# Placing v by small transfers and repeating e on TensorE, in a fused attention and soft-MoE kernel

## The chip, the cores and the metric

The kernel runs on one core of a Trainium2 chip. The time is the device time of one launch in microseconds (us). A core has five engines that run side by side and meet at semaphores: PE (TensorE, matrix products; its weight loads are listed as PEld), DVE (VectorE), ACT (ScalarE), POOL (GpSimd) and SP (SyncE, which here only issues transfers). Transfers run on 16 DMA engines. A transfer that casts its data is issued by POOL and shows up as queue q0 in the profile; transfers issued by SP are queue q1.

## The reference

```python
def _attn_ref(q, k, v, cap):              # q, k, v: (8, 12, 448, 64) float32
    scores = (1 / sqrt(64)) * q @ k^T
    scores = cap * tanh(scores / cap)     # cap = 30
    attn = softmax(scores)
    return attn @ v

def _moe_ref(x, phi, w1, w2):             # x: (3584, 768), phi: (768, 32)
    logits = x @ phi                      # w1: (8, 768, 1024), w2: (8, 1024, 768)
    d = softmax(logits over tokens)       # per slot
    slot_input = (d.T @ x).reshape(8, 4, 768)
    for e in range(8):
        slot_out[e] = relu(slot_input[e] @ w1[e]) @ w2[e]
    c = softmax(logits over slots)        # per token
    return c @ slot_out
```

The attention output, with its heads side by side, is the `x` of the mixture. All inputs and the output are float32; the kernel computes in bf16 with sums in float32.

## The kernel before

The 96 heads are taken in 24 groups of four, called quads (`Q`). A quad holds two head pairs (`pr = 2 Q + h`), and the two heads of a pair lie on the two halves of the 128 partitions. A pair's 448 keys are cut into 7 pieces of 64, so that one tile of scores has 64 keys of each of two heads on its partitions and 448 queries along the row. Six such tiles make a chunk `j`; there are 56 chunks.

A loop over the chunks is the spine of the kernel. In chunk `j`, ACT takes tanh of two halves of scores (L324) and exp of the chunk before (L328); PE computes the scores of the next chunk (`qk_chunk`, L315) and, for a pair whose exponentials are complete, the product with v (`pv_first`, `pv_tail`, `pv_rest`, L586); DVE normalises it into `xq` (L596) and computes part of the exponentials as polynomials (L560 to L568). The order on each engine is written out by hand: `at(j, slot, f, ...)` hangs further work into a slot of a chunk ("0", "m", "e", "a", "b", "r", "c", "d"), `run(j, slot)` issues it, and a table `WHEN` gives slots for the transposes of k and q (L275), the transposes of x, the logits, the exponentials e of the logits, and their sums. PE also gets matmuls whose result nobody reads (L616, L829, L832).

v enters the product through two block-diagonal tiles, `vbds[0]` and `vbds[1]`, taken in turn by the quads. A row has 2 x 7 pieces of `VW = 130` values: 64 values of v of the first head and a one, then 64 of the second head and a one. On partitions 0 to 63 only the first half of a piece is filled, on 64 to 127 only the second; zeros and ones are written once (`init_vbd`). v is loaded as float32 into one staging tile, `vraw`, in two transfers of 64 partitions (`load_v`, issued by SP, L195), and `vcast` (L285) copies it on POOL into `vbds[Q % 2]`, cast to bf16, one half of the partitions at a time. `vcast_after(pr)`, behind the product of each pair, issues these casts; ahead of one of them POOL writes a zero into one column (L293).

POOL issues all transfers that cast: k and q of later quads (`load`, L185, two tiles of each) and 64 pieces of the weights (`wjobs`): 32 of `w1` and 11 of `w2` into on-chip tiles and 21 of `w2` into a copy in DRAM (`w2d`), which SP reads back behind the attention (`w2t`, L1015). The pieces are spread over the chunks.

Per batch of 12 heads (three quads) there are logits for 32 slots (`phib`, loaded once in 128-byte pieces), and their exponentials `es[b]`, 128 tokens by 4 groups by 32 slots. `e_rep` (L679) copies `es[b]` on POOL four times side by side into `e4s[b]`. `e_norm` (L687) multiplies `e4s` with a column of ones to add up e over the tokens, and `e_transp` (L698) transposes it: in both the four copies land on four blocks of 32 partitions. Behind the attention come the two expert layers (L1036, L1069) and the combination (L1107, L1158), whose results SP stores.

Of the kernel before, what the change touches and what calls it, by code (L numbers as in the profile page):

```python
# [9 lines left out]
F32 = mybir.dt.float32  # L10
BF16 = mybir.dt.bfloat16
# [7 lines left out]
P = 128  # L19
HP = 64  # L20
NT = 7
DH = 64
S = 448
CH = 6
CS = 3
NG = 4
NF = 3
NEX = 5
TAIL = NF * P
W = DH + 1  # L30
# [7 lines left out]
def kernel(  # L38
# [12 lines left out]
    B, H, _, _ = q.shape  # L51
    D = H * DH
    E = moe_w1.shape[0]
    F = moe_w1.shape[2]
    NS = moe_phi.shape[1]
# [7 lines left out]
    NQ = B * NQB  # L63
# [6 lines left out]
    pe, dve, act, pool, sp = nc.tensor, nc.vector, nc.scalar, nc.gpsimd, nc.sync  # L70

    consts = ctx.enter_context(tc.tile_pool(name="consts", bufs=1))
    wts = ctx.enter_context(tc.tile_pool(name="wts", bufs=1))
# [4 lines left out]
    ones = wide[:, 0:P]  # L78
    dve.memset(ones, 1.0)
    ident = consts.tile([P, P], BF16, name="ident")  # L80
# [5 lines left out]
    half1 = consts.tile([P, 1], BF16, name="half1")  # L86
# [55 lines left out]
    ldv, wk = homes["ldv"], homes["wk"]  # L142
# [21 lines left out]
    raws, casts, qkT = {}, {}, {}  # L164
# [3 lines left out]
    def quad_ap(nm, Q, h=None):  # L168
        b, hq = divmod(Q, NQB)
        off = (b * H + 4 * hq) * S * DH  # L170
        if h is not None:
            return bass.AP(tensor=srcs[nm].tensor, offset=off + 2 * h * S * DH,
                           ap=[[NT * DH, P], [1, NT * DH]])
        return bass.AP(tensor=srcs[nm].tensor, offset=off,
                       ap=[[NT * DH, P], [2 * S * DH, 2], [1, NT * DH]])
# [9 lines left out]
            pool.dma_start(out=t, in_=quad_ap(nm, Q))  # L185
            raws[nm, Q] = t

    vraw = ldv.tile([P, 2, S], F32, name="vraw")

    def load_v(Q, n):  # L190

        if Q < NQ:
            r = slice(n * HP, n * HP + HP)
            src = quad_ap("v", Q)
            sp.dma_start(out=vraw[r],  # L195
                         in_=bass.AP(tensor=src.tensor, offset=src.offset + n * S * DH,
                                     ap=[[NT * DH, HP]] + list(src.ap[1:])))
            raws["v", Q] = vraw

    def load_first():  # L200

        for nm in "qk":
            raws[nm, 0] = [ld.tile([P, S], F32, name=f"{nm}raw{h}", tag=nm + "raw", bufs=2)
                           for h in range(2)]
        raws["v", 0] = vraw
        kc = raws["k", 0][0].rearrange("p (c d) -> p c d", d=DH)
        kin = quad_ap("k", 0, 0).rearrange("p (c d) -> p c d", d=DH)
        sp.dma_start(out=raws["q", 0][0], in_=quad_ap("q", 0, 0))
        for c0, c1 in ((0, CS), (CS, NT)):
            act.dma_start(out=kc[:, c0:c1, :], in_=kin[:, c0:c1, :])  # L210
        for nm in "kq":
            sp.dma_start(out=raws[nm, 0][1], in_=quad_ap(nm, 0, 1))
        t = wts.tile([P, 3, 2, S], F32, name="raw1", tag="w1", bufs=E)
        t01 = wts.tile([P, 2, 2, NT, P], BF16, name="casts", tag="w1", bufs=E)
        for n, nm in enumerate("kqv"):
            raws[nm, 1] = t[:, n, :, :]
            if nm != "v":
                for Q in range(2):
                    casts[nm, Q] = t01[:, n, Q, :, :]
            if nm == "v":  # L220
                sp.dma_start(out=raws["v", 0], in_=quad_ap("v", 0))
            sp.dma_start(out=raws[nm, 1], in_=quad_ap(nm, 1))
# [59 lines left out]
    def vcast(Q, n):  # L282
        raw = raws["v", Q].rearrange("p h (c d) -> p h c d", d=DH)
        r, c0 = slice(n * HP, n * HP + HP), n * W
        pool.tensor_copy(vbds[Q % 2][r, :, :, c0:c0 + DH], raw[r])  # L285
        if Q != 1:
            load_v(max(Q + 1, 2), n)

    def vcast_after(pr):

        Q, h = divmod(pr, 2)
        if h == 0 and 1 < Q + 1 < NQ:
            pool.memset(vbds[Q % 2][HP:P, h, NT - 1, 0:1], 0.0)  # L293
            vcast(Q + 1, 1)
        elif h == 1 and Q + 2 < NQ:
            vcast(Q + 2, 0)

    def init_vbd(n):
        t = vbds[n]
# [366 lines left out]
        for hq in range(NQB):  # L666
            xTs.pop(b * NQB + hq)

    es, e4s = {}, {}

    def e_exp(b):
        es[b] = consts.tile([P, NG, NS], BF16, name="E", tag="E", bufs=2)
        act.activation(es[b], lps.pop(b), ACT.Exp)
        e_rep(b)

    def e_rep(b):

        e4s[b] = consts.tile([P, NG, 4 * NS], BF16, name="e4", tag="e4", bufs=1)
        pool.tensor_copy(e4s[b].rearrange("p g (a s) -> p g a s", a=4),  # L679
                         es[b].unsqueeze(2).to_broadcast([P, NG, 4, NS]))  # L680

    def e_norm(b):

        ps = psT.tile([P, 1], F32, name="zps", tag="T")
        for g in range(NG):
            r = slice(0, P if g < NF else HP)
            pe.matmul(ps, e4s[b][r, g, :], ones[r, 0:1], start=(g == 0), stop=(g == NG - 1))  # L687
        if b == 0:
            dve.tensor_copy(zacc, ps)
        else:  # L690
            dve.tensor_tensor(zacc, ps, zacc, op=ALU.add)

    def e_transp(b):

        ps = psT.tile([P, 512], BF16, name="eps", tag="T")
        for g in range(NG):
            n = P if g < NF else HP
            pe.transpose(ps[:, g * P:g * P + n], e4s[b][0:n, g, :], ident[0:n, 0:n])  # L698
        dve.tensor_copy((ETl if b >= B - 2 else ET4[:, b // 2])[:, :, b % 2, :],
                        ps[:, 0:S].rearrange("p (c q) -> p c q", q=HP))  # L700

# [42 lines left out]
    def at(j, slot, f, *a):  # L744
        if j < 0:
            j, slot = 0, "b"
        aux.setdefault((j, slot), []).append((f, a))
# [63 lines left out]
    at(1, "c", init_vbd, 1)  # L811
    for n in range(2):
        at(0, "d", vcast, 0, n)

    def run(j, slot):
        for part in ("<", "", ">"):
# [29 lines left out]
    for j in range(NCH):  # L846
        run(j, "0")
        tanh_chunk(2 * j)
        if j == NCH - 1:
            exp_chunk(j - 1)  # L850
        run(j, "m")
        tanh_chunk(2 * j + 1)
        run(j, "e")
        if j < 2:
            exp_chunk(j)
        elif 2 < j < NCH - 1:
            exp_chunk(j - 1)
        pr = pair_at.get(j - 2)
        if pr is not None:
            pv_first(pr)  # L860
        run(j, "a")
        if pr is not None:
            pv_tail(pr, 0, CA)
        if j == NCH - 1:
            pv_rest(pr)
            break
        qk_chunk(2 * j + 2)
        run(j, "b")
        if pr is not None:
            pv_rest(pr, aux.pop((j, "r"), ()))  # L870
            vcast_after(pr)
        else:
            run(j, "r")
        run(j, "c")
        qk_chunk(2 * j + 3)
        run(j, "d")
# [71 lines left out]
        tail_step(*step)  # L948
    assert not aux, aux.keys()

    el = consts.tile([P, NG, NS], BF16, name="E", tag="E", bufs=2)
    es[bl] = el
    xpl = [bank([P, 2 * P], BF16, name="xpl"),
           psT.tile([P, 2 * P], BF16, name="xpl", tag="T")]
    zl = bank([P, 1], name="zps")

    def z_last(b):
        for g in range(NG):
            n = P if g < NF else HP
            if b < bl:  # L960
                pe.matmul(zl, e4s[b][0:n, g, :], ones[0:n, 0:1], start=(g == 0), stop=False,
                          skip_group_check=True)
                continue
            for a in range(4):
                pe.matmul(zl[32 * a:32 * a + NS, :], es[b][:, g, :],
                          ones[:, 0:1] if g < NF else half1, start=False, stop=(g == NG - 1),
                          skip_group_check=True)

    def x_last(s, copy):
        q0, q1 = 2 * s * P, min(2 * s * P + 2 * P, S)  # L970
# [21 lines left out]
    for s in range(2):  # L992
        js = slice(3 * s, 3 * s + 3)
        slot_mms(bl, sl_ps, (NF,), range(3 * s, 3 * s + 3))
        dve.tensor_tensor(slT[:, js, :], sl_ps[s], slacc[:, js, :], op=ALU.add)
    e_rep(bl)
    z_last(bl)
    junk = bank([P, 3 * P], name="junk")
    for a in range(0, P, NS):
# [144 lines left out]
    for n in range(B // 2 * NT):  # L1144
        bb, c = divmod(n, NT)
        if n == NH + 3:
            e_transp(B - 1)
            e_rep(B - 2)
        if n == NH + 5:
            e_transp(B - 2)  # L1150
        if n == NH + 7:
            e_sums(B // 2 - 1)
        op = fin.tile([P, 2, 512], F32, name="op", tag="op")
        if n < NH:
            half_tile(n, 1, op[:, 0, 0:HD], "act" if n % 2 else "dve")
            continue
        for half in range(2):
            pe.matmul(op[:, half, 0:HD], et_tile(bb, c), so[half],  # L1158
                      start=True, stop=True)

        if n == NH or c == 0 or full:
            ob, n1 = wts.tile([P, 2, 2, HD], F32, name="ob", tag="w1", bufs=E), n
        dst = ob[:, n - n1, :, :]
        if n % 2:
            dve.tensor_scalar_mul(dst, op[:, :, 0:HD], winv[:, bb, c:c + 1])
        else:
            act.mul(dst, op[:, :, 0:HD], winv[:, bb, c:c + 1])
        full = n > n1 or c == NT - 1
        if full:
            store(n1, 0, 2, ob[:, 0:n - n1 + 1, :, :].rearrange("p t a d -> p (t a d)"),  # L1170
                  n - n1 + 1)
# [35 lines left out]
```

## Time and profile before

| | |
|---|---|
| times of three runs | 294.11, 294.23, 294.27 us, median 294.23 |
| span of the profiled execution, first to last instruction | 292.0 us |
| time of the profiled execution | its span and about 2.2 us around it (294.23 less 292.0) |
| busy: PE, DVE, ACT, POOL | 254.3, 242.2, 255.4, 138.8 us |
| mean granted TensorE clock | 0.978 |
| DMA packets, bytes moved | 57614, 68.11 MB |
| read from and written to DRAM | 91.72 MB, 19.27 MB |
| q0 (issued by POOL), q1 (issued by SP) | 42448 and 14832 packets |
| casts of v on POOL (L285) | 46 of `vraw`, 952 ns each in the median, and 2 of the second quad |
| copies of e on POOL (L679) | 9, 609 ns each in the median |

Busy times come from one profiled execution; engines overlap, so they do not add up to the span. Attention fills the span up to some 246 us; the two expert layers and the stores of the output fill the rest. Line numbers (L285) are those of the kernel before. The share of a DMA queue is the time that its packets took, added up and divided by 16 times the stretch; since packets of one engine overlap, shares may add up to more than 100%.

### The profile page before, as it was taken

To read this page: it belongs to the slowest core of one execution; us is meant where nothing else is said; L and a number is where in the kernel's file an instruction comes from. 1 tells how busy PE (TensorE), PEld (TensorE's weight loads), DVE (VectorE), ACT (ScalarE), POOL (GpSimd) and SP (SyncE) were. 2 spreads that over 40 slices of the span, in tenths; PEclk is the share of its full clock that TensorE was granted. 3 is DMA by queue.
4 is the path that set the end of the run, shared out by engine and by line. 5 is a ranking of instruction groups with operands and counts; after the bars stand their busy time and mean duration, and the time that the engine had idled before them with its cause. 6 is when DMAs were issued, how large, how long until landed. Compare 5 with 4: busy or idle time off the path is not lost.

```text
span 292.0 us, 10785 instructions
## 1 busy us (share of the span) xinstructions
PE 254.3 (87%) x4728; PEld 173.3 (59%) x4728; DVE 242.2 (83%) x505; ACT 255.4 (87%) x208; POOL 138.8 (48%) x200
## 2 busy tenths in 40 slices
PE   8898789989998999899889998999899899998620
PEld 6555466757675767576657675767576668543300
DVE  3727899999999999999999999999989985257740
ACT  4999999999999999999989999999999997236620
POOL 4492645774675467655845566465553220300000
PEclk9999999999999999999999999999999999999965
DMA  7999999999999999999999999999999568979995
GB/s 237 244 190 204 205 186 217 216 212 217 221 226 186 211 230 232 197 209 230 214 203 197 216 212 204 213 228 227 197 187 229 125 226 275 406 282 339 418 427 237
DMA packets 57614, 68.11 MB, mean 233 GB/s; under 512 B 4064, under 2 KB 53472, under 8 KB 57568
## 3 DMA queue, kind: packets, MB, share of 16 engines
q0 software_dynamic: 42448, 35.31, 78.0%
q1 hardware_dynamic: 14832, 31.89, 31.1%
q8 instruction: 37, 0.61, 0.8%
q10 hardware_dynamic: 288, 0.23, 0.2%
q14 instruction: 9, 0.07, 0.1%
HBM read 91.72 MB, written 19.27 MB: 380 GB/s over the span
## 4 chain that ended last, share of the span: by engine, by line
DVE 48%; PE 33%; ACT 8%; DMA 3%; POOL 2%; issue 2%; DVEq 0%; ACTq 0%; SPq 0%
PE pv L586 11%; DVE xq L596 8%; PE sc L315 5%; DVE ex L567 5%; DVE xp L566 4%; DVE xT L648 4%; ACT ex L328 3%; DVE xf L562 3%; DVE xp L564 3%; ACT ex L324 3%; DVE ex L560 3%; DVE ex L568 3%; PE pv L616 3%; DVE qT L277 3%; DVE xp L563 2%; DVE kT L277 2%
## 5 line engine op out<-in xcount | busy, mean ns | idle before, releaser
L324 ACT ACTIVATE ex<-sc 128x1344 f16<-128x1344 f32 (+1 forms) x113 | 142.2, 1320 | 2.6 <-PE sc L315 2.4
L328 ACT ACTIVATE ex<-ex 128x2688 bf16<-128x2688 f16 (+5 forms) x58 | 110.3, 1906 | 0.1
L586 PE MATMUL pv<-vbd,ex 128*128 128x130 bf16 (+1 forms) x1610 | 95.1, 212 | 7.6 <-POOL vbd L285 4.7
L586 PEld LDWEIGHTS <-ex 128*128 128x128 bf16 (+1 forms) x1680 | 75.7, 101 | 36.0 <-PE sc L315 7.7
L315 PE MATMUL sc<-qT,kT 64*64 64x448 bf16 x672 | 70.8, 360 | 1.0 <-ACT ex L324 0.7
L285 POOL CAST vbd<-vraw 64x896 bf16<-64x896 f32 x46 | 44.2, 960 | 45.8 <-PE pv L586 29.6
L596 DVE TENSOR_TENSOR xq<-pv,rec 128x448 bf16<-128x448 f32 x46 | 28.7, 624 | 1.5
L315 PEld LDWEIGHTS <-kT 64*64 64x64 bf16 x672 | 23.4, 105 | 6.8 <-issue 5.4
L293 POOL MEMSET vbd<- 64x1 bf16 x22 | 4.0, 180 | 46.4 <-PE pv L586 46.4
L117 POOL DMA_DIRECT2D w1b<-in_moe_w_dram x32 | 25.0, 782 | 0.0
L566 DVE TENSOR_TENSOR xp<-xp,xf 128x1344 f16<-128x1344 f16 (+2 forms) x33 | 23.6, 715 | 0.9
L564 DVE TENSOR_TENSOR xp<-xp,xf 128x1344 f16<-128x1344 f16 (+2 forms) x33 | 23.8, 722 | 0.2
L567 DVE TENSOR_TENSOR ex<-ex,xp 128x1344 uint16<-128x1344 uint16 (+2 forms) x33 | 23.3, 705 | 0.4
L679 POOL COPY e<-E 128x512 bf16<-128x512 bf16 x9 | 6.2, 693 | 34.0 <-PE eps L698 17.6
L616 PE MATMUL pv<-ones 128*128 128x57 bf16 x474 | 18.6, 188 | 0.0
L185 POOL DMA_DIRECT2D qb<-in_q_dram x22 | 16.8, 766 | 3.1 <-DMA kraw<-in_k_dram 3.1
L277 DVE COPY kT<-kps 128x896 bf16<-128x896 bf16 x23 | 14.2, 617 | 4.5 <-PE kps L275 4.3
L275 PE MATMUL qps<-ident,qb 128*64 128x128 bf16 x308 | 12.8, 222 | 5.3 <-DVE xT L648 5.3
L563 DVE TENSOR_SCALAR xp<-xf 128x1344 f16<-128x1344 uint16 (+2 forms) x33 | 16.5, 501 | 0.2
L275 PEld LDWEIGHTS <-qb 128*64 128x64 bf16 x308 | 10.1, 109 | 10.8 <-issue 10.4
L560 DVE TENSOR_SCALAR ex<-ex 128x1344 uint16<-128x1344 f16 (+2 forms) x33 | 16.4, 498 | 0.0
L616 PEld LDWEIGHTS <-ones 128*128 128x128 bf16 x474 | 16.2, 96 | 0.0
(135 smaller groups left out, 360.7 us busy)
## 6 DMA issues: line engine op xcount, KB each, us to landing
w1b<-in_moe_w_dram POOLq DMA_DIRECT2D x32, 384.0 KB, 8.8
vraw<-in_v_dram SPq DMA_DIRECT2D x44, 224.0 KB, 6.2
w2d<-in_moe_w_dram POOLq DMA_DIRECT2D x21, 384.0 KB, 8.9
w2t<-w2d SPq DMA_DIRECT2D x21, 384.0 KB, 6.8
out_dram<-ob SPq DMA_DIRECT2D x9, 768.0 KB, 7.6
qb<-in_q_dram POOLq DMA_DIRECT2D x22, 224.0 KB, 7.6
kb<-in_k_dram POOLq DMA_DIRECT2D x22, 224.0 KB, 6.1
w2b<-in_moe_w_dram POOLq DMA_DIRECT2D x11, 384.0 KB, 8.8
```

Source lines behind the costliest of these rows:

```text
L277: dve.tensor_copy(t, ps)
L285: pool.tensor_copy(vbds[Q % 2][r, :, :, c0:c0 + DH], raw[r])
L315: pe.matmul(sc[cs, u, 0:S], qkT["k", Q][r, c, cs], qkT["q", Q][r, :, cs], start=True, stop=True)
L324: act.activation(exs[j][:, half * CS + u0:half * CS + u1, :].bitcast(F16), sc[:, u0:u1, 0:S], ACT.Tanh, scale=qk_scale / cap)
L328: act.activation(exs[j][:, u0:u1, :], exs[j][:, u0:u1, :].bitcast(F16), ACT.Exp, scale=cap)
L560: lambda: dve.tensor_scalar(y, t.bitcast(F16), octaves * STEP, base * STEP + c0, ALU.mult, ALU.add),
L564: lambda: dve.tensor_tensor(p, p, f, op=ALU.mult),
L566: lambda: dve.tensor_tensor(p, p, f, op=ALU.mult),
L567: lambda: dve.tensor_tensor(y, y, p, op=ALU.add),
L586: pe.matmul(out_, exs[j][r, u, q0:q0 + (HP if tail else P)], v_, start=(c == 0 and g == gs[0] < NF), stop=(c == NT - 1), skip_group_check= ...
L596: dve.tensor_tensor(xq[Q][:, h, s0:s1, :], pv[:, 0:s1 - s0, 0:DH], rec.to_broadcast([P, s1 - s0, DH]), op=ALU.mult)
L616: pe.matmul(home, ones, ones[:, 0:512 - NT * W], start=False, stop=True, skip_group_check=True)
```

## The change

v is loaded by POOL, one cast transfer per quad, into a bf16 staging tile `vst` (two buffers). For quads 2 to 23, `place_v` then has SP copy it from there into the block-diagonal tile: four transfers per quad (two halves of the partitions, two head pairs), each of 64 partitions x 7 runs of 64 bf16 values (128 bytes). Both are issued behind the products of the pairs: behind the second pair of quad Q, quad Q + 2 is placed; behind the first, quad Q + 3 is loaded. Only quads 0 and 1 are still cast by POOL. The float32 v of quad 0 moves into the third part of the tile `casts`.

`e_rep` and `e4s` are gone. `z_mms` (for `e_norm` and `z_last`) and `e_transp` run each of their four matmuls four times, once for each block of 32 partitions, from `es[b]` itself, of which there are three buffers now.

```diff
-    vraw = ldv.tile([P, 2, S], F32, name="vraw")
-
-    def load_v(Q, n):
+    def load_v(Q):
         if Q < NQ:
-            r = slice(n * HP, n * HP + HP)
-            src = quad_ap("v", Q)
-            sp.dma_start(out=vraw[r],
-                         in_=bass.AP(tensor=src.tensor, offset=src.offset + n * S * DH,
-                                     ap=[[NT * DH, HP]] + list(src.ap[1:])))
-            raws["v", Q] = vraw
+            raws["v", Q] = ldv.tile([P, 2, S], BF16, name="vst", tag="vst", bufs=2)
+            pool.dma_start(out=raws["v", Q], in_=quad_ap("v", Q))
+
+    def place_v(Q):
+        if 1 < Q < NQ:
+            t = raws.pop(("v", Q)).rearrange("p h (c d) -> p h c d", d=DH)
+            for n in range(2):
+                r, c0 = slice(n * HP, n * HP + HP), n * W
+                for h in range(2):
+                    sp.dma_start(out=vbds[Q % 2][r, h, :, c0:c0 + DH], in_=t[r, h])
...
         pool.tensor_copy(vbds[Q % 2][r, :, :, c0:c0 + DH], raw[r])
-        if Q != 1:
-            load_v(max(Q + 1, 2), n)
-
-    def vcast_after(pr):
+
+    def v_after(pr):
         Q, h = divmod(pr, 2)
-        if h == 0 and 1 < Q + 1 < NQ:
-            pool.memset(vbds[Q % 2][HP:P, h, NT - 1, 0:1], 0.0)
-            vcast(Q + 1, 1)
-        elif h == 1 and Q + 2 < NQ:
-            vcast(Q + 2, 0)
+        if h:
+            place_v(Q + 2)
+        else:
+            load_v(Q + 3)
...
     def e_exp(b):
-        es[b] = consts.tile([P, NG, NS], BF16, name="E", tag="E", bufs=2)
+        es[b] = consts.tile([P, NG, NS], BF16, name="E", tag="E", bufs=3)
         act.activation(es[b], lps.pop(b), ACT.Exp)
-        e_rep(b)
-
-    def e_rep(b):
-        e4s[b] = consts.tile([P, NG, 4 * NS], BF16, name="e4", tag="e4", bufs=1)
-        pool.tensor_copy(e4s[b].rearrange("p g (a s) -> p g a s", a=4),
-                         es[b].unsqueeze(2).to_broadcast([P, NG, 4, NS]))
+
+    def z_mms(b, ps, first, last):
+        for g in range(NG):
+            for a in range(4):
+                pe.matmul(ps[32 * a:32 * a + NS, :], es[b][:, g, :],
+                          ones[:, 0:1] if g < NF else half1, start=(first and g == 0),
+                          stop=(last and g == NG - 1), skip_group_check=True)
...
-            pe.transpose(ps[:, g * P:g * P + n], e4s[b][0:n, g, :], ident[0:n, 0:n])
+            for a in range(4):
+                pe.transpose(ps[32 * a:32 * a + NS, g * P:g * P + n], es[b][0:n, g, :],
+                             ident[0:n, 0:n])
...
+    at(1, "a", load_v, 2)
...
-            vcast_after(pr)
+            v_after(pr)
```

More of the change, by code (lines that the diff above doesn't have):

```diff
@@ L204, in load_first @@
                            for h in range(2)]
-        raws["v", 0] = vraw
         kc = raws["k", 0][0].rearrange("p (c d) -> p c d", d=DH)
@@ L213, in load_first @@
         t = wts.tile([P, 3, 2, S], F32, name="raw1", tag="w1", bufs=E)
-        t01 = wts.tile([P, 2, 2, NT, P], BF16, name="casts", tag="w1", bufs=E)
+        both = wts.tile([P, 3, 2, S], F32, name="casts", tag="w1", bufs=E)
+        t01 = both[:, 0:2, :, :].rearrange("p a b s -> p (a b s)").bitcast(BF16).rearrange(
+            "p (a b c d) -> p a b c d", a=2, b=2, d=P)
+        raws["v", 0] = both[:, 2, :, :]
         for n, nm in enumerate("kqv"):
@@ L667, in logits @@
             xTs.pop(b * NQB + hq)
-    es, e4s = {}, {}
+    es = {}
     def e_exp(b):
-        es[b] = consts.tile([P, NG, NS], BF16, name="E", tag="E", bufs=2)
+        es[b] = consts.tile([P, NG, NS], BF16, name="E", tag="E", bufs=3)
         act.activation(es[b], lps.pop(b), ACT.Exp)
-        e_rep(b)
-    def e_rep(b):
-        e4s[b] = consts.tile([P, NG, 4 * NS], BF16, name="e4", tag="e4", bufs=1)
-        pool.tensor_copy(e4s[b].rearrange("p g (a s) -> p g a s", a=4),
-                         es[b].unsqueeze(2).to_broadcast([P, NG, 4, NS]))
+    def z_mms(b, ps, first, last):
[4 more added lines that the diff above has]
+                          stop=(last and g == NG - 1), skip_group_check=True)
     def e_norm(b):
         ps = psT.tile([P, 1], F32, name="zps", tag="T")
-        for g in range(NG):
-            r = slice(0, P if g < NF else HP)
-            pe.matmul(ps, e4s[b][r, g, :], ones[r, 0:1], start=(g == 0), stop=(g == NG - 1))
+        z_mms(b, ps, True, True)
         if b == 0:
@@ L949 @@
     assert not aux, aux.keys()
-    el = consts.tile([P, NG, NS], BF16, name="E", tag="E", bufs=2)
+    el = consts.tile([P, NG, NS], BF16, name="E", tag="E", bufs=3)
     es[bl] = el
@@ L957, in z_last @@
     def z_last(b):
[L958 to L967, printed above, removed]
+        z_mms(b, zl, b < bl, b == bl)
     def x_last(s, copy):
@@ L995 @@
         dve.tensor_tensor(slT[:, js, :], sl_ps[s], slacc[:, js, :], op=ALU.add)
-    e_rep(bl)
     z_last(bl)
@@ L1147 @@
             e_transp(B - 1)
-            e_rep(B - 2)
         if n == NH + 5:
```

## The prediction

> **What bounds the kernel now.** I first read the busy times in stretches of 20 us. Columns: stretch, length, busy us (and instructions) of PE, PEld, DVE, ACT and POOL, granted clock, DMA share, GB/s.
>
> ```profile
> 100.00:120.00 20.00, 18.60 (x401) 13.60 (x397) 19.39 (x40) 19.75 (x16) 11.02 (x16) 1.00 1.22 226
> 120.00:140.00 20.00, 19.09 (x365) 12.75 (x360) 19.47 (x39) 20.00 (x16) 12.10 (x18) 1.00 1.24 210
> 140.00:160.00 20.00, 17.43 (x372) 12.64 (x370) 19.55 (x38) 18.86 (x15) 12.01 (x18) 1.00 1.21 205
> ```
>
> ACT never rests: 178.2 us of the 180 from 40 to 220 us. It is the bound there, so work taken from POOL or DVE can give back at most the missing 1.8 us. POOL, which the change relieves, is busy 60% of the time. The DMA share is above 1, so I asked for the DMA queues in three windows: a pure backlog (20 to 27 us), the window of the 64-byte packets of `phib` (11.6 to 13.1 us), and the attention stage (40 to 220 us). Columns: packets, MB, share of 16 engines.
>
> ```profile
> DMA packets 1500, 1.43 MB, mean 204 GB/s; under 512 B 66, under 2 KB 1499, under 8 KB 1499
> q0 software_dynamic: 1499, 1.41, 123.4%
> ```
> ```profile
> DMA packets 959, 0.28 MB, mean 187 GB/s; under 512 B 705, under 2 KB 959, under 8 KB 959
> q0 software_dynamic: 949, 0.26, 167.2%
> ```
> ```profile
> DMA packets 40170, 38.06 MB, mean 211 GB/s; under 512 B 2014, under 2 KB 40136, under 8 KB 40136
> q0 software_dynamic: 34952, 29.30, 104.7%
> q1 hardware_dynamic: 5184, 8.26, 14.9%
> q8 instruction: 27, 0.44, 0.9%
> ```
>
> Packets overlap: with a backlog the 16 engines show 124.2% (123.4 and 0.8 of q8). The stage shows 120.6% over its 180 us, so the DMA engines are some 97% full (120.6/124.2). The packet records, fitted over the 160 whole microseconds with 16 or more packets open, give 80 ns of an engine for a q0 packet that writes 1024 B, 74 for 896 B, 61 for 768 B, 83 for a 1792 B packet of `v` on q1; by these the engines are 95% full. So idle DMA time from 20 to 221 us is 3 to 5%, 6 to 10 us; I take 8. What covers it is the slack of the loads:
>
> ```profile
> L185 POOL DMA_DIRECT2D kb<-in_k_dram x22: 702/742/751, 5.9 to 210.1; - x22
> DMA to landing us min/median/max: 4.3/6.1/9.3
> ```
>
> From each landing to its first transpose the trace leaves 3.8 to 9.3 us for `kb` and 2.7 to 8.4 us for `qb` (the last `qb`: lands 221.0, used 224.7). ACT and the DMA engines are thus two limits, 1% and 3 to 5% from full.
>
> **Part 1, casts leave POOL.** 44 casts x 952 ns (L285), 22 memsets (4.0 us) and 9 copies of e (6.2 us, L679) go, 52 us of POOL; 22 loads of `v` x 0.74 us (the rows of `kb`) come, 16 us. POOL does not bound the stage, and this gives nothing by itself. The stall that ends with it is small:
>
> ```profile
> PE pv L586 <- POOL vbd L285: 4.7, 14, 0.7
> ```
>
> These 14 waits end in PE's own fill matmuls, while ACT stays busy: 0. DVE gains too: L568 at 128x1344 took 499 ns without and 743 ns with a cast beside it. ACT decides, so 0 again, 1.8 us at best.
>
> **Part 2, v comes by POOL's queue.** 22 loads of 256 packets leave q1 (83 ns) for q0 (74 ns): 21 x 256 x 9 / 16 = 3.0 us of DMA time saved until the last loads. The 44 SP issues (595 ns) become 88; SP mostly waits (196 us for POOL and `vraw`): 0. On SP the `w2t` loads queue behind the last placement, free to go at 233.5 us; only three of the 21 were issued earlier (230.7 to 231.9), and the tenth lands at 250.0 for a use at 256.3: 0, uncovered up to 1. The first placement is wanted at 41 us and free to go at 27: 0.
>
> **Part 3, placement.** Each group of four heads gets four transfers of 64 x 7 runs of 128 B, 1792 packets, 112 on each engine. No 128 B copy between on-chip tiles is in the trace. The nearest row is `phib`: 128 B read, 64 B written. Its window had 675 such packets, and 254 large ones at 75 ns; 16 x 1.5 us less 254 x 75 ns leaves 4.95 us, 7.4 ns each, the lower bound. Upper bound: the time recorded for one, 27 ns, with nothing overlapped. I take 11 ns, near the row of throughput, a little more because twice the bytes are written and the runs begin at odd offsets (steps of 260 B). 21 groups x 112 x 11 ns = 25.9 us (17.4 to 63.5). The Trainium skill, "DMA: Bandwidth & Descriptors", section "Why small descriptors are slow (HBM only)", says that copies inside SBUF don't suffer from short packets: 128 B packets reach 78% of the link. At the 27 GiB/s per engine under "Specifications" that would be an estimated 5.7 ns, 13.3 us, and by it the sum below would show no excess beyond the slack.
>
> Sum for the DMA engines: 25.9 - 3.0 - 8 idle = 14.9 us too much by the last `qb`. Its slack takes 3.7 us; 11.2 us are left, and PE's transposes, the scores, then ACT wait for them.
>
> **Part 4, new waits.** `load_v(Q+3)` on POOL waits for the four placements of Q+1 (`vst` has two buffers); `kb`, `qb` and weight jobs queue behind. From the pv rows, `vbd` of quad Q is free 9.0, 10.1 or 14.1 us before pv of Q+2 wants it (a cycle of three). With a backlog q0 and q1 alternate packet by packet (packet records at 107 us: 25 to 28 of each queue in 250 ns), so a transfer of 28 packets per engine takes 28 x (75 + 11) = 2.4 us. A first pair waits for the first and third transfer. The first can go before the second head pair is done, so two remain, 4.8 us, and about 2.5 us of issue and landing (least landing of `vraw`: 3.3 with 8 packets per engine): 7.3 of 9.0 us. Covered, 0; the cover gone, each us beyond costs one us in two groups of three, 15 in all. `load_v` is released some 9.7 us after `vbd` was free, about 5 us behind its place in the order; the loads behind it lose about 5 us, which eats most of their slack. That is why I count no slack beyond 3.7 us.
>
> **Part 5, e on TensorE.** 12 more transposes per batch at 73 ns (six of L634 take 0.44 us on the chain) and 12 more one-column matmuls at 12 ns (16 of L965 take 0.19 us): 1.0 us in each of six batches. In those chunks scores are ready 0.9 to 1.3 us before ACT wants them, and PE idles 1.5 of 20 us: 0, uncovered up to 6. After attention 12 one-column matmuls stand on the chain: +0.15 us; the 24 transposes near 268 us lie beside the output DMA: 0 to 1.8, I take 0.
>
> **Sum.** The profiled execution has a span of 292.0 us; the three times have a median of 294.23, so 2.2 us lie around the span. 294.2 + 11.2 + 0.15 = 305.6, rounded to 305. With 7.4 ns per packet it is 297, with 27 ns 343.
>
> **The rivals.**
> - Costly small packets (chance 0.17). If a placed packet keeps its engine for up to 27 ns, the excess rises to 52 us, 343; halfway, 17 to 19 ns, about 322. Two transfers then take 5.7 us, so pv starts to wait as well. For it: destinations at odd offsets. Against: `phib`'s 7.4 ns. The Trainium skill, "DMA: Bandwidth & Descriptors", "Specifications", says that below 512 B the engines do read-modify-write; that speaks for this case, and no run here shows it yet.
> - Hidden (0.13). At 7 ns per packet and 10 us idle, 16.5 - 3.0 - 10 = 3.5 us are too much, and the slack of 3.7 us covers them: 294 to 296. For it: `phib`'s 7.4 ns, if placing costs no more. Against: every idle stretch would have to be filled, while POOL now waits about 5 us per group at `load_v`. The Trainium skill's rule on copies inside SBUF (part 3) speaks for this case.
> - Faster (0.10). The placements fit, the exclusion between casts and DVE goes, PE loses its 4.7 us of waits, and ACT's 1.8 us of gaps close: 292.4 at best, 293. It decides if a placed packet costs under about 6 ns. For it: DVE stands for 48% of the chain. Against: ACT's 99%.
>
> **Numbers.** The forecast, the DMA engines overfilled and attention stretched by 4 to 25 us, has 0.60; its own range is 298 to 320. 0.2% (0.6 us) is about what a measurement of this kernel can tell from no change. Faster 0.10; same 0.08, from the hidden case; slower 0.60 + 0.17 + 0.05 = 0.82. From 294 to 326 leaves out the faster case and the upper half of the costly one, about 0.19.
>
> **What would show it.** Right: DMA slices at 9 throughout, q1 with some 50,000 packets, waits of PE or PEld for DMA `kb`, `qb` or `vst`, gaps on ACT before L324, POOL waiting for DMA at `load_v`, the attention stage some 11 us longer, the part behind it unchanged. Waits of pv for `vbd` DMA in front of those on `kb` and `qb` would mean the costly case. ACT still at 99% means hidden or faster. The prediction is wrong if attention stretches while the DMA engines have idle time, or if the small packets take under 6 ns.

## The result, and the profile after

The changed kernel takes 324.21 us (median; 320.42 to 327.87) against 294.25 for the kernel before on the same chip: a ratio of 1.092 [1.089, 1.095]. It is slower, as forecast, but by 27 us by this ratio, where 11 were forecast. Its profiled execution has a span of 318.6 us. (Two of its four runs, 326.23 and 327.87 us, fell in a slower state; medians are over all runs, while ratios, and the losses worked out from them, use undisturbed runs alone.)

The last tanh of attention starts at 268.9 us, against 241.3 before; from there to the end it is 49.7 and 50.7 us. So the whole loss is in attention. The same three stretches of 20 us as before, same columns:

```profile
100.00:120.00 20.00, 15.88 (x315) 11.76 (x316) 13.83 (x29) 16.30 (x13) 5.98 (x8) 0.91 1.22 173
120.00:140.00 20.00, 16.20 (x313) 11.72 (x311) 16.66 (x34) 17.11 (x13) 7.63 (x10) 0.92 1.38 193
140.00:160.00 20.00, 18.33 (x401) 13.26 (x400) 17.12 (x35) 16.74 (x13) 8.78 (x12) 1.00 1.24 169
```

ACT, busy 99% before, is down to 16 to 17 us of 20. No engine has become the bound instead: DVE and POOL are busy for less time than before in all three stretches, and PE in the first two (in the third it has 18.33 us against 17.43). The DMA engines move 169 to 193 GB/s where they moved 205 to 226. And another column matters now: the granted clock, 1.00 before, falls to 0.91. Next, the DMA queues from 40 to 220 us:

```profile
DMA packets 63913, 33.26 MB, mean 185 GB/s; under 512 B 31188, under 2 KB 63884, under 8 KB 63884
q0 software_dynamic: 34195, 29.16, 106.6%
q1 hardware_dynamic: 29689, 3.67, 22.2%
```

The small packets are there. By the prices of the forecast for the larger packets, the full microseconds (16 or more packets open) leave 9.2 ns of an engine for one of 128 B; the records say 21 ns each, overlaps included. By these prices, work for the DMA engines fills about 89% of 20 to 250 us, against 95% of 20 to 221 us before: they have idle time, and the transfers are late all the same. The page's rows of issues (KB of one, median us to landing) say that a load of `kb` takes 8.3 us, where it took 6.1 before, and a placement 7.8:

```profile
kb<-in_k_dram POOLq DMA_DIRECT2D x22, 224.0 KB, 8.3
...
vbd<-vst SPq DMA_DIRECT2D x88, 56.0 KB, 7.8
```

The table of waits (us in total, times, longest) of the changed kernel names the new ones (PEld and PE stand side by side in the same wait, so their rows are not to be added):

```profile
POOL vst L192 <- DMA vbd<-vst: 145.2, 19, 14.3
ACT ex L326 <- PE sc L317: 23.0, 18, 4.6
...
PEld L280 <- DMA kb<-in_k_dram: 15.3, 6, 3.8
...
PE kps L280 <- DMA kb<-in_k_dram: 12.8, 5, 3.4
...
PEld L280 <- DMA qb<-in_q_dram: 10.9, 8, 2.9
```
```profile
SPq L201 <- DMA vst<-in_v_dram: 100.0, 19, 13.0
```

POOL stands 145 us at `load_v` (L192) for placements, 7.6 us each time. It issues every load of k and q behind that. SP in turn waits 100 us at `place_v` (L201) for the staged v that POOL loaded late. The chain of waits from 125 to 160 us shows one turn of this circle (start, us, what):

```profile
116.94 9.53 DMA vbd<-vst
...
127.03 0.73 POOL vst L192
127.77 8.95 DMA kb<-in_k_dram
136.71 0.04 issue
136.76 0.96 PE kps L280 x11
...
150.91 0.62 SPq L201
...
151.62 10.32 DMA vbd<-vst
```

A placement lands at 126.5 us; only then POOL can load v and, behind it, k. That k lands at 136.7 us and PE starts on it within 0.1 us: it had stood idle since 134.0. In the kernel before the same load was issued at 112.7, landed at 118.6 and was used at 123.0. Over the run, the time from the landing of `kb` to its use fell from 3.8 to 9.3 us to 0.0 to 9.9, and 8 of 22 have 0.6 us or less; of `qb`, 15 of 22 have 1.0 us or less.

### The profile page after: what moved, and what is told of

Read it like the earlier page. It is cut to its first block, busy times and chain, and to the rows that moved or that the text cites. A ratio compares the mean times of both kernels' runs of the same rounds, so it can differ in the third digit from the quotient of the medians.

```text
span 318.6 us, 11203 instructions
## 1 busy us (share of the span) xinstructions
PE 262.6 (82%) x4908; PEld 179.3 (56%) x4908; DVE 237.1 (74%) x505; ACT 257.5 (81%) x208; POOL 104.5 (33%) x147
## 3 DMA queue, kind: packets, MB, share of 16 engines
q1 hardware_dynamic: 49328, 26.85, 34.6%
## 4 chain that ended last, share of the span: by engine, by line
PE 34%; DMA 34%; DVE 14%; ACT 10%; issue 2%; POOL 2%; SPq 1%; DVEq 0%; POOLq 0%; ACTq 0%
DMA vbd<-vst 19%; PE pv L588 11%; DMA kb<-in_k_dram 7%; DMA qb<-in_q_dram 6%; PE sc L317 5%; ACT ex L326 4%; ACT ex L330 4%; DVE xq L598 2%; PE kps L280 2%; PE pv L618 2%; PE so_ps L1063 2%; PE hp L1030 2%; PE op L1151 1%; DVE xp L566 1%; PE qps L280 1%
## 5 line engine op out<-in xcount | busy, mean ns | idle before, releaser
L588 PE MATMUL pv<-vbd,ex 128*128 128x130 bf16 (+1 forms) x1610 | 99.1, 217 | 6.9 <-DVE xq L598 3.6
L588 PEld LDWEIGHTS <-ex 128*128 128x128 bf16 (+1 forms) x1680 | 79.0, 104 | 36.3 <-DVE xq L598 12.5
L317 PE MATMUL sc<-qT,kT 64*64 64x448 bf16 x672 | 72.6, 366 | 0.6 <-ACT ex L326 0.4
L192 POOL DMA_DIRECT2D vst<-in_v_dram x22 | 16.1, 731 | 145.2 <-DMA vbd<-vst 145.2
L282 DVE COPY kT<-kps 128x896 bf16<-128x896 bf16 x23 | 14.3, 623 | 17.8 <-PE kps L280 17.3
L282 DVE COPY qT<-qps 128x896 bf16<-128x896 bf16 x23 | 14.3, 620 | 14.9 <-PE qps L280 14.8
L568 DVE TENSOR_TENSOR xp<-xp,xf 128x1344 f16<-128x1344 f16 (+2 forms) x33 | 23.4, 708 | 0.9
L280 PE MATMUL kps<-ident,kb 128*64 128x128 bf16 x308 | 13.3, 227 | 12.8 <-DMA kb<-in_k_dram 12.8
L618 PE MATMUL pv<-ones 128*128 128x57 bf16 x474 | 22.0, 202 | 0.0
L280 PEld LDWEIGHTS <-kb 128*64 128x64 bf16 x308 | 9.5, 112 | 21.0 <-DMA kb<-in_k_dram 15.3
L618 PEld LDWEIGHTS <-ones 128*128 128x128 bf16 x474 | 19.6, 106 | 0.0
L650 DVE COPY xT<-xps 128x896 bf16<-128x896 bf16 (+1 forms) x24 | 14.4, 599 | 4.0 <-PE xps L641 4.0
## 6 DMA issues: line engine op xcount, KB each, us to landing
w1b<-in_moe_w_dram POOLq DMA_DIRECT2D x32, 384.0 KB, 10.2
```

Source lines behind the costliest of these rows:

```text
L280: pe.transpose(ps[h * HP:h * HP + HP, c, :], src[:, h, c * DH:(c + 1) * DH], ident)
L282: dve.tensor_copy(t, ps)
L317: pe.matmul(sc[cs, u, 0:S], qkT["k", Q][r, c, cs], qkT["q", Q][r, :, cs], start=True, stop=True)
L568: lambda: dve.tensor_tensor(p, p, f, op=ALU.mult),
L588: pe.matmul(out_, exs[j][r, u, q0:q0 + (HP if tail else P)], v_, start=(c == 0 and g == gs[0] < NF), stop=(c == NT - 1), skip_group_check= ...
L618: pe.matmul(home, ones, ones[:, 0:512 - NT * W], start=False, stop=True, skip_group_check=True)
```

## The experiments

**Theory A** (the chain): placing is slow from issue to landing, and stands in a circle of two staging buffers: v is loaded when a placement has landed, and loads of k and q queue behind on POOL. **Theory B** (the load): 39,424 small packets take more of the DMA engines than is free, as the forecast had it.

**Each part alone.** `e_only`, run twice, is the kernel before with the part on e as in the diff of the change; `v_only` is the changed kernel with the same part undone (the signs turned round).

```diff
-        e_rep(b)                  # four copies on POOL
...
-            pe.matmul(ps, e4s[b][r, g, :], ones[r, 0:1], start=(g == 0), stop=(g == NG - 1))
+        z_mms(b, ps, True, True)  # four matmuls for each, from es[b]
```

> The kernel before with only the e part of the change (matmuls and transposes from es itself, no copies of e on POOL); v still comes as before. All theories put the loss into the placing of v, so each expects 294.0 to 295.0 us here. A value over 296 us would mean that the 24 extra small matmuls per batch cost PE something on the path.

> The kernel before with only the e part, a second time, for a profile beside that of before: 291.5 to 293.0 us. If the 2 us come from the attention stage, ACT's idle time from 40 to 220 us falls from 1.8 us to under 1 us; if from the last stage, attention ends at 238 us as before and the rest gets shorter.

> The changed kernel without the part on e: v staged and placed as in the changed kernel (two buffers, four transfers per quad in the changed kernel's order), e copied four times by POOL as before. Theory A (the staging chain of v is the whole cost, and the part on e saves its 2 us only where ACT has no stalls, as when it was run alone): 322 to 328 us, no different from the changed kernel's 324.2 within its own spread of 7 us. Rival (once PE has stalled, the 24 more small matmuls of each batch stand on the path, so the part on e adds to the loss): 316 to 321 us, below the changed kernel by 3 or more, with fewer stretches of the half-speed clock.

`e_only`: 292.14 us (291.1 to 295.8), ratio 0.993 [0.991, 0.995]; again 292.00, ratio 0.993 [0.991, 0.995]. Alone it is faster by 2 us, which was not expected. `v_only`: 327.58 us (326.3 to 330.2), ratio 1.116 [1.111, 1.120]. So all of the loss is v's. The part on e is a gain alone, and beside v's part too, if 1.116 is set against the changed kernel's 1.092 (the two come from separate measurements). On the chain its matmuls cost less than the +0.15 us of the forecast. The sums behind attention that have 4 matmuls before and 16 in `e_only_again` take:

```profile
246.59 0.16 PE zps L961 x4
```
```profile
246.25 0.19 PE zps L679 x16
```

That is +0.03 us; the second sums, 2.4 us later, have 16 matmuls in both kernels. Where the gain comes from is only partly seen: from the last tanh to the end it takes 49.9 us instead of 50.7 (and 49.7 in the changed kernel against 50.9 in `v_only`), and attention ends 0.4 us earlier. No single wait accounts for it.

**Few packets, same waits.** `long_runs` places each head's 448 values in one run, 64 packets per transfer instead of 448. They land in other columns than those meant for them, so the product is computed from other values; all waits and bytes stay.

```diff
-                    sp.dma_start(out=vbds[Q % 2][r, h, :, c0:c0 + DH], in_=t[r, h])
+                    row = vbds[Q % 2][r, h].rearrange("p c w -> p (c w)")
+                    sp.dma_start(out=row[:, n * S:n * S + S], in_=t[r, h].rearrange("p c d -> p (c d)"))
```

> The changed kernel with each placing transfer writing one run of 448 values per partition (896 B, 64 packets) instead of 7 runs of 64 (448 packets); the number of transfers and all waits stay. The values then lie in the wrong places of the block-diagonal tile, so the result of attention is wrong; what is computed and moved in bytes is the same. Theory A: a placing transfer lands in about 3 us instead of 7.8, load_v is released early, POOL's wait falls under 60 us, 295 to 300 us. Theory B: the engines lose only about 0.4 us of work per quad, 10 us in all, so 308 to 316 us. Theory C: pv no longer waits, 295 to 300 us.

293.97 us (292.5 to 298.8), ratio 0.999 [0.996, 1.002]. The loss is gone; theory B had expected 308 to 316. Its row of issues and its stretch from 40 to 220 us:

```profile
vbd<-vst SPq DMA_DIRECT2D x88, 56.0 KB, 5.3
```
```profile
40.00:220.00 180.00, 164.75 (x3477) 116.05 (x3479) 172.20 (x348) 177.31 (x136) 78.28 (x106) 1.00 1.26 211
```

POOL still waits 106.7 us for placements here (theory A had expected under 60), but what stands behind is hardly late: a long wait on POOL is not yet a loss. The DMA share is 1.26, above what the forecast took for full (1.24): full engines alone cost nothing here either. This run takes away both the small packets' load and their latency, so it doesn't tell A from B.

**The load alone.** `long_plus_small` adds to `long_runs` the same number of small packets, written by SP to a tile that no other engine reads or waits for; the product is again computed from other values, as in `long_runs`.

```diff
             place_v(Q + 2)
+            small_packets(Q + 2)     # 4 transfers of 64 x 7 runs of 128 B, to a tile "extra"
```

> The kernel of the run with long placing runs (values in the wrong places of the tile, so the result is wrong), plus the 39,424 small packets again: behind each four placing transfers SP issues four transfers of 64 x 7 runs of 128 B from the tile of ones into a tile that nobody reads. The DMA engines carry as many small packets as in the changed kernel, but no instruction of attention waits for them. Theory A (waiting for small-packet transfers costs the time, not their load on the engines): 294 to 299 us. Theory B (load): 308 us or more. Theory C makes the same forecast as A.

312.40 us (310.1 to 314.3), ratio 1.062 [1.057, 1.068]. It failed to separate the theories: in the trace SP's transfers land in the order of issue, so the placements stood behind the small packets of the quad before (one set of placements lands at 122.9 to 124.5 us, right behind small packets that landed at 122.4). They took 7.8 us to land again, and POOL waited 122 us. It shows only that small packets ahead in the queue bring a loss too, 18 us here.

**Less load, same chain.** `changed_light` leaves 22 of the 64 weight loads out (other weights are used in their place), about 43 us of DMA time. `vst_three_light` does the same with three staging buffers.

```diff
+    for e in (1, 3, 5):
+        w1b[e] = w1b[e - 1]
...
-        at(1 + n * (NCH - 5) // len(wjobs), "b", *job)
+        if job:
+            at(1 + n * (NCH - 5) // len(wjobs), "b", *job)
```

> The changed kernel, two staging tiles, with the same 22 weight loads left out (the result is wrong in the same way). Theory A' (the placing packets alternate with a backlog on q0, which makes a placement slow and so holds load_v): with less backlog a placing transfer lands in 4 to 6 us instead of 7.8, POOL's wait at load_v falls under 110 us, and the time to 296 to 308 us. If the time were set by the order of the waits alone, whatever the load: 315 us or more.

> The kernel with three staging tiles, with 22 of the 64 weight loads left out (experts 1, 3 and 5 use the first-layer weights of 0, 2 and 4, and every second spilled piece of w2 is that of its neighbour, so the result is wrong; all matmuls stay). That takes 22 x 1.95 us = 43 us of DMA time out of the attention stage and leaves the small packets as they are. If the 9 us that three tiles leave against the e part alone (301.1 to 292.1) are the DMA engines' lack of room (theory B for this rest): 291.5 to 294 us, engines no longer full. If they are the placements' own latency (theory C): 297 us or more, with pv still waiting for vbd.

`changed_light`: 311.93 us (307.95 to 320.1), ratio 1.054 [1.046, 1.063]; `vst_three_light`: 306.04 (301.0 to 312.3), ratio 1.029 [1.019, 1.039], no better than with all loads (next). With far more free DMA time than is missing by theory B, 16 and 8 us of loss stay. What the changed kernel gains, 11 us, can be engines' time or the shorter queue of POOL behind `load_v`; this pair doesn't tell.

**Another place in the order.** `v_load_late` issues the load of v behind the second head pair, where its buffer is nearly free, so that k and q don't queue behind the wait.

```diff
             place_v(Q + 2)
-        else:
             load_v(Q + 3)
```

> The changed kernel with load_v(Q+3) issued on POOL behind the second pair of quad Q instead of the first, right behind place_v(Q+2); transfers, packets and tiles are the same. Theory A (head of line: load_v waits on POOL for the placements of Q+1, and the loads of k and q queue behind it, so they land late): POOL's wait at load_v falls from 145 us to under 40, PE's waits for kb and qb (47 us) nearly vanish, 295 to 301 us. Theory B (the DMA engines are overfilled by 39,424 small packets): the same bytes and packets must pass, 312 to 324 us. Theory C (placed late: pv itself waits for vbd): no change, 318 to 326 us.

311.48 us (309.4 to 312.3), ratio 1.059 [1.056, 1.062]. That lies outside the ranges of all three theories: over A's 295 to 301, just under B's 312 and C's 318. The waits of PE on k and q are gone, and another has come:

```profile
POOL vst L192 <- DMA vbd<-vst: 116.4, 17, 13.3
PE pv L587 <- DMA vbd<-vst: 16.4, 8, 5.0
```

v itself is now late, and the product waits for its placement. POOL still waits 116 us, where theory A had expected under 40. With two buffers, one or the other was late in both orders.

**A third staging buffer.** `vst_three` gives `vst` a third buffer (room from an unused padding tile and from the third buffer of `es`).

```diff
-            raws["v", Q] = ldv.tile([P, 2, S], BF16, name="vst", tag="vst", bufs=2)
+            raws["v", Q] = ldv.tile([P, 2, S], BF16, name="vst", tag="vst", bufs=3)
```

> The changed kernel with three staging tiles vst instead of two (room for it from an unused padding tile and from two instead of three buffers of e); packets, transfers and their order stay. load_v(Q+3) then waits for the placements of Q, two quads back, and not of Q+1. Theory A (head of line: POOL and the loads behind load_v wait for placements): POOL's wait falls from 145 us to under 30, PE's waits for kb and qb vanish, 295 to 303 us. Theory B (the DMA engines have no room for the small packets): 308 us or more, engines with 16 packets open at nearly all times. Theory C (placements themselves come too late for pv): pv waits for vbd, 310 us or more, POOL not waiting.

301.08 us (299.1 to 303.5), ratio 1.025 [1.018, 1.031]: 20 of the 27 us are back, with every small packet in place. The waits of PE for `kb` and `qb` are gone; the product waits, 8.9 us in all:

```profile
POOL vst L191 <- DMA vbd<-vst: 78.1, 14, 9.7
...
PE pv L587 <- DMA vbd<-vst: 8.9, 6, 2.2
```

**No staging.** `direct_cast` has POOL cast v straight from DRAM into the block-diagonal tiles, four transfers per quad.

```diff
-                    sp.dma_start(out=vbds[Q % 2][r, h, :, c0:c0 + DH], in_=t[r, h])
+                    pool.dma_start(out=vbds[Q % 2][r, h, :, c0:c0 + DH], in_=...)   # v in DRAM
```

> The changed kernel without staging: POOL issues four casting transfers per quad straight from DRAM into the block-diagonal tile (64 x 7 runs, 256 B read, 128 B written), at the place where the placements were issued; no vst, no placements by SP. The DMA engines then carry 39,424 packets of 256 B instead of 5,632 of 1792 B, estimated from 1792 B at 74 ns less 17 x 4 ns of small-packet cost at about 14 ns each, 34 us against 26 us. POOL waits for PE as in the kernel before, and the third transfer lands some 10 us behind the release of vbd, where pv wants it after 9 to 14 us. If the staging chain is the main loss (theory A): 293 to 300 us. If small packets are the loss wherever they are issued (theory B): 305 us or more.

306.05 us (302.7 to 308.0), ratio 1.035 [1.027, 1.043]. Without the staging circle it still loses 10 us, which is in theory B's range (305 or more) and not in A's (293 to 300). The product waits 7.8 us for `vbd`, about as with three buffers. But it is a different load: by the same fit as above its casting packets leave about 24 ns of an engine each, where 14 were expected; that is an estimate of 59 us for the 39,424 of them instead of 34. So it says nothing against the circle, and its own loss may well be the engines'; no run separates that.

**The order of the four placements.** In the changed kernel the first head pair needs the first and the third transfer, and the second transfer waits for the second pair's product. `by_pair` exchanges the two loops of `place_v`, so that the first pair's two transfers go first and wait only for the first pair's product; `three_by_pair` does so with three buffers.

```diff
-            for n in range(2):
-                r, c0 = slice(n * HP, n * HP + HP), n * W
-                for h in range(2):
+            for h in range(2):
+                for n in range(2):
+                    r, c0 = slice(n * HP, n * HP + HP), n * W
```

> The changed kernel with the two loops of place_v exchanged, so that both transfers of the first head pair stand ahead of those of the second on SP. Packets, bytes and issues are the same. Theory A (the placing transfers, in series between the products and the next load of v, hold the loop): the first two can go as soon as the first pair's product is done, some 5 us earlier; behind the second pair two transfers are left, not three, so POOL's waits at load_v fall from 145 to about 100 us, k and q are late less often, and the time lies at 305 to 315 us. Theory B (the load on the DMA engines by small packets sets the time, whatever the order): within 1% of the changed kernel's 324, 320 to 328.

> The kernel with three staging buffers (301.1 us) with the two loops of place_v exchanged. Theory A: what is left there is the product that waits for the placing of its own tile (8.9 us in 6 waits, and the half-speed clock behind them); the first pair needs two transfers instead of three, and these are released about 5 us earlier, so the waits of pv for vbd fall under 2 us, and the time to 292 to 296 us, near the kernel with the part on e alone (292.0). Theory B (the transfers are slowed by the load and something else than their place in the order sets the last 9 us): 299 to 303, waits of pv unchanged in sum.

`by_pair`: 317.73 us (317.0 to 320.7), ratio 1.079 [1.069, 1.088]. It gains 4 of the 27 us, less than theory A had expected (305 to 315): POOL still waits 123.9 us for placements (about 100 were expected), since its buffer is free only when the fourth has landed. `three_by_pair`: 293.75 us (291.1 to 297.0), ratio 0.989 [0.980, 0.999], within what theory A expected. The loss is gone with the same packets, bytes and issues as in the changed kernel. Its three stretches of 20 us, its waits of POOL for placements, and its rows of issues:

```profile
100.00:120.00 20.00, 19.12 (x414) 13.68 (x411) 19.38 (x40) 19.91 (x16) 8.23 (x11) 1.00 1.43 214
120.00:140.00 20.00, 18.36 (x372) 12.33 (x370) 19.50 (x40) 20.00 (x16) 9.35 (x13) 1.00 1.49 213
140.00:160.00 20.00, 17.58 (x392) 12.58 (x390) 17.93 (x36) 19.83 (x16) 8.91 (x13) 1.00 1.50 213
```
```profile
POOL vst L191 <- DMA vbd<-vst: 30.7, 7, 5.2
```
```profile
kb<-in_k_dram POOLq DMA_DIRECT2D x22, 224.0 KB, 11.7
...
vbd<-vst SPq DMA_DIRECT2D x88, 56.0 KB, 8.8
```

ACT is back at 99%, with the DMA engines full and the transfers of attention landing later after their issue than in the changed kernel (11.7 us for `kb`, 8.8 for a placement). What differs is that the loads are issued early enough and that the first pair's placement goes first. Here the larger packets leave 5.5 ns of an engine for a small one.

One table for the cause. The third column is the time from `vbd` being free (the start of the last matmul of the quad two back) to the landing of the first pair's placement, median of 21 quads; "gaps" are PE's idle stretches of over 1.2 us before the last tanh, with their number; "half speed" is the time there at a granted clock of 0.5.

| kernel | us | ratio | first pair lands after | gaps, us | ACT idle after 40 us | half speed, us |
|---|---|---|---|---|---|---|
| before | 294.25 | 1 | | 0 | 1.9 | 0 |
| changed | 324.21 | 1.092 | 9.7 | 20.3 (9) | 27.8 | 23.9 |
| `by_pair` | 317.73 | 1.079 | 5.8 | 17.3 (7) | 22.6 | 17.1 |
| `vst_three` | 301.08 | 1.025 | 9.8 | 7.1 (4) | 10.2 | 13.7 |
| `three_by_pair` | 293.75 | 0.989 | 5.9 | 1.4 (1) | 1.2 | 0 |
| `long_runs` | 293.97 | 0.999 | 4.8 | 1.9 (1) | 2.7 | 0 |

Two waits were to be undone, and each kernel of the middle undoes one: the third buffer frees POOL (k and q come in time), the order of the loops brings the first pair's v in time. Only both together give all of it, and they leave every packet as it was, so the load by itself is not the cause.

The last columns show a third thing. ACT loses more than PE stands still: 27.8 against 20.3 us. In the trace of the changed kernel six of the nine gaps are followed by 3.4 or 6.8 us at a clock of 0.5 (gap 134.0 to 136.8 us, half speed from 136.6 for 3.4 us). That is up to 12 us of TensorE's time, and in `three_by_pair`, with one gap of 1.4 us, there is none. The Trainium skill, "TensorE: Matmul & The Clock Gate", Part 1, says that the clock drops to half after at least one idle window of some 3.4 us, and comes back after a busy one. The steps of 3.4 us agree; by the gaps measured here a whole idle window is not needed, since those that were followed by half speed lasted 1.7 to 3.39 us, less than one step of 3.41. How much of the loss is the clock's was not separated by a run.

## Why the prediction was right or wrong

**Direction: right; size: too small; mechanism: wrong in its main term.** The forecast was 305 (294 to 326), the result 324, or 321 by the ratio. It named most signs rightly: waits of PE for `kb` and `qb`, gaps on ACT before the tanh, POOL waiting at `load_v`, q1 at 49,328 packets, the part behind attention unchanged. Two signs failed: attention stretched by 27.6 us and not some 11, and the DMA engines did not stay full. It also named what would make it wrong, "if attention stretches while the DMA engines have idle time", and that is what the trace shows.

- *What bounds the kernel now, part 1 and part 2*: ACT's limit and the DMA engines' fill were read rightly. What the casts' leaving POOL and the saving of part 2 bring by themselves was not run. One row was misread: the 743 ns of L568 are not beside a cast of v. They are the mean of the six that ran beside a copy of e (L679), four of 0.86 us and two of 0.51. No price hung on it.
- *Part 3, placement*: the price was near in the changed kernel, 11 ns taken and 9.2 measured, and twice too high in `three_by_pair` (5.5). With 5.5 the forecast's own sum has 12.9 - 3.0 - 8 = 1.9 us of excess, which the slack of 3.7 covers; with 9.2 it has 6.9 left of the 11.2. But that is not what the changed kernel lost: its engines have idle time, `three_by_pair`, with the same small packets, loses nothing, and with 43 us of DMA time taken out `changed_light` still loses 16. Of the 11.2 us of this term the runs show none.
- *The Trainium skill's rule on copies inside SBUF* ("DMA: Bandwidth & Descriptors", "Why small descriptors are slow (HBM only)"): an estimate of 5.7 ns from it stood against 11. The measured 5.5 to 9.2 ns agree with its direction, and no run gave placed packets the 27 ns of the costly rival. Whether the read-modify-write below 512 B, which the Trainium skill states under "Specifications" there, is part of the 9.2 ns is not shown. By that rule the sum gave no excess, which was right for the load and would have been wrong for the kernel.
- *Part 4, new waits*: here is the step that failed, the one priced at 0. It said 7.3 us from a free `vbd` to the first pair's placement, under a window of 9.0, 10.1 or 14.1. Measured: 9.7. The transfers pass as forecast (2.4 us each; in `three_by_pair` the two of the first pair land 1.6 to 2.9 us apart, 2.2 in the median); so the part for issue and landing, taken as 2.5 from the 3.3 us of `vraw`'s quickest load, is 4.9 by the same sum (`long_runs`, where the transfers themselves are short, still takes 4.8 in all). The product itself hardly waits for it in the changed kernel (0.4 us, once), because k and q are later still. The release of `load_v`, forecast 9.7 us after `vbd` is free, came at 11.7. And the wait was priced once, about 5 us that eat the slack of the loads behind. It comes back: late v makes late placements, and these make the next v late, so POOL waited 7.6 us on average and 14.3 at most. In the trace: placements land at 126.5 us, the next v is loaded from 127.0 to 135.5, and SP places it from 135.5 on. Slack is spent once; a circle asks for it in every turn.
- *Nothing for the clock*: the forecast took a microsecond of stall as a microsecond of time. Behind six of the eight stalls of PE over 1.7 us stand 3.4 us or more at half speed.
- *Part 5, e on TensorE*: the sums behind attention went from 0.16 to 0.19 us, where +0.15 was forecast. The whole part was a gain of 2 us, where a cost of 0 to 6 was given.
- *Rivals*: "costly small packets" had a time near the result (322) but its mechanism, an engine kept for 17 to 19 ns, is refuted; its sign, waits of pv in front of those on `kb`, is seen only in `v_load_late`, `vst_three` and `direct_cast`. "Hidden" is what the same packets do in `three_by_pair`. "Faster" did not come; e alone is 0.7% faster, but not by the way that this rival names.

## What to carry to other kernels

When a copy on an engine is replaced by a transfer, count the latency from release to landing, and follow it round: which buffer does it hold, which load waits for that buffer, and what is queued behind that load. If the circle is longer than the work it hides under, it is late in every turn, and free DMA engines do not mend that by themselves (here 16 us of loss stayed with 43 us of their work taken out); another buffer, and the piece that is wanted first ahead in the queue, took back all 27 us at the same packets and bytes. Ask of each stall of TensorE whether the clock falls behind it. For this kernel the part on e alone is the plain version to keep (ratio 0.993 [0.991, 0.995]); with v placed by transfers as well, `three_by_pair` (0.989 [0.980, 0.999]) does no harm, and a gain beyond that of e is not shown.

## What the runs showed of the hardware that was not expected

- A copy between on-chip tiles in 128 B packets costs an engine 5.5 to 9.2 ns per packet in full stretches, if the larger packets keep their prices of before, while each is recorded with 21 to 25 ns. The same pieces cast straight from DRAM by POOL's queue (`direct_cast`) leave about 24 ns each by that fit.
- Time to landing can grow while nothing is late: `kb` took 6.1 us before, 8.3 in the changed kernel and 11.7 in `three_by_pair`, which loses nothing.
- Gaps of PE as short as 1.7 us were followed by half the clock, in steps of 3.4 us; in the same trace gaps of 2.1 and 2.5 us (at 64.6 and 115.2 us) were not. The length alone doesn't decide it. In every trace with several changes of the clock they lie on one grid with steps of 3.41 us, and the clock follows how long PE stands idle within one step: in the 14 traces, of the 831 steps at full clock between 40 us and the last tanh, all 23 with over 1.9 us of idle PE were followed by half the clock, none of the 776 with under 1.2 us, and 14 of the 32 between. The grid cuts the gap of 2.5 us at 115.2 us into 0.9 and 1.6.
